# Fixing the order of ScalarE, VectorE and GpSimd in the expert part of an attention and mixture-of-experts kernel, with preparation in small lots

## The chip, the core and the metric

The kernel runs on one NeuronCore of a Trainium2 chip. The metric is the device time of one execution in microseconds (us). The engines are called as the profile calls them: PE (TensorE matrix multiply), PEld (its weight loads), DVE (VectorE), ACT (ScalarE), POOL (GpSimd) and SP (SyncE, whose queue issues every DMA here). "Lnnn" is a line of the kernel before, unless it is said to be of the changed one.

## What is computed

The reference chains three blocks on 1152 tokens (2 batches of 576) with width 512:

```python
out = attention(q, k, v, M_prev, z_prev, beta)       # causal, 8 heads of 64, gated with a memory read
x = out.transpose(0, 2, 1, 3).reshape(1152, 512)
a, b = x @ w1, x @ w2                                # 512 -> 1024
x = (a * b @ w3) @ w_out                             # 1024 -> 1024 -> 512
...
p = domain_probs / (domain_probs.sum(-1, keepdims=True) + 1e-09)
for e in range(4):                                   # the expert part
    h = np.maximum(x @ moe2_w1[e], 0.0)              # 512 -> 1024
    out += p[:, e:e + 1] * (h @ moe2_w2[e])          # 1024 -> 512
```

## The kernel before

Every matrix is split into a high half (rounded to the matmul format) and a low half (what is left), and a product is three matmul passes: high by low, low by high, high by high. ACT makes high halves (`hi`, a CAST), POOL or DVE the low halves (`lo_pool`, line 80; `lo_dve`, line 83, a subtraction).

The expert part is a loop over 32 steps: expert e (4), column block c (the 1152 tokens in two blocks, 2x320 and 2x256 columns), and a quarter j of the 1024 hidden features. `step(s, segs)` makes the first layer of a quarter by a seven-product scheme on 2x2 blocks. Its products write three PSUM tiles, Z, Q and R. In order: Z (A11 by B11), R (A12 by B21), Z again (S2 by T2), half of Q (S1 by T1), Z (S3 by T3), the other half of Q, Z (A22 by T4), Q (S4 by B22). Between them ACT copies Z out (s1, u2, u3), since the next product adds onto the same bank, and DVE adds the parts (t11, t22, t12). `relu_split` then makes the two halves of the hidden tile he: the high half on ACT, the low half on DVE. For A22 by T4 both halves are read from the Z bank itself, so the next step's first product waits for DVE's low half there. Between the products stand five segments of other PE work: in step 0 the last matmuls of the block before (`c1_rest`, L507), in all others the second layer of the step before (`layer2`, the matmuls into o, L741, 30 of them after a 320 block and 24 after a 256 block, and after each fourth quarter the additions into acc on DVE).

Work that has to be ready ahead of a step:

- `combine_x(c)`: the sums T1 to T4 of the tokens' blocks and the halves of T1 to T4 and B22, on ACT and DVE. For c = 0 it is needed from step 0's third product on, for c = 1 from step 4 on.
- `prep_1(s)`: the first layer's weights of step s. The raw tile r1 (two buffers) is loaded by `load_1` from SP, POOL forms sums in place (`s31`, `s24`, four operations of 256 columns), ACT and POOL make the halves `hi`/`lo` of four tiles w10 to w13: A11 and A12 in w10, S2 and S4 in w11, S1 and A22 in w12, S3 in w13.
- `prep_2(s)`: the second layer's weights w2, two `hi` on ACT and two `lo` on DVE, from r2, loaded by `load_2`.

What sets the order: only PE keeps the order of the program text (`manual_schedule` with PE alone). For ACT, DVE, POOL and SP the framework's scheduler lists each engine's instructions by its own estimate when the kernel is built; on the chip each engine then works through its list in order. The text feeds preparation through a queue (`pop`, line 779): up to four items after each segment, items for up to two steps ahead. The normalisation of the probabilities (10 small loads into `pr`, four DVE operations, L837 to L841) stands at the start of the expert part.

Of the kernel before, what the change touches and what calls it, by code (L numbers as in the profile page):

```python
# [33 lines left out]
def kernel(  # L34
# [34 lines left out]
    GAPB = 648  # L69
# [543 lines left out]
    def prep_1(s):  # L613


        if s >= len(steps):
            return []
# [29 lines left out]
        return [begin, hi(0), lo(0), s31, s24, hi(1), hi(2), lo(1), hi(3), lo(2), lo(3)]  # L647

    def prep_2(s):
        if s >= len(steps):  # L650
            return []
        st = {}

        def begin():
# [5 lines left out]
        return [  # L660
            begin,
            *(lambda x=x: nc.scalar.copy(w2s[s][x][:, 0], st["r"][:, x]) for x in range(2)),  # L662
            *(lambda x=x: lo_dve(w2s[s][x][:, 1], st["r"][:, x], w2s[s][x][:, 0]) for x in range(2)),
        ]
# [48 lines left out]

    def rows_of(t):

        c, i = divmod(t, TILES)
        t0, w = COLS[c]
        spans = []
        for b in range(B):
            lo, hi = max(i * P, b * w), min((i + 1) * P, (b + 1) * w)  # L720
            if lo < hi:
                spans.append((lo - i * P, hi - i * P, b * S + t0 + lo - b * w))
        return spans
# [51 lines left out]
    queue = []  # L775

    later = []

    def pop(s, n):
        while n and queue and queue[0][0] <= s + 2:  # L780
            queue.pop(0)[1]()
            n -= 1
        if later:
            later.pop(0)()

# [110 lines left out]
```

## Time and profile before

| | |
|---|---|
| time, median of 3 runs (lowest, highest) | 752.51 us (752.22, 752.82) |
| the profiled execution: its time, its span | 753.2 us, 751.4 us |
| granted TensorE clock, mean over the span | 0.991 |
| share of the span busy: PE, PEld, DVE, ACT, POOL | 96%, 86%, 56%, 51%, 48% |
| the chain that ended last, by engine | PE 83%, ACT 4%, DVE 4%, POOL 3%, DMA 3%, issue 2% |
| DMA | 73.55 MB, mean 98 GB/s |

The profiled execution's time is 1.8 us more than its span, and 0.7 us above the median. A granted clock of 1 stands for 2.4 GHz and 0.5 for 1.2 GHz. Matmuls are pipelined and their ends are modelled, so a share of 96% does not say that PE is at its peak; the length of a step, from the first product of one to that of the next, is the surer measure.

### The profile page before, as it was taken

To read this page: it belongs to the slowest core of one execution; us is meant where nothing else is said; L and a number is where in the kernel's file an instruction comes from. 1 tells how busy PE (TensorE), PEld (TensorE's weight loads), DVE (VectorE), ACT (ScalarE), POOL (GpSimd) and SP (SyncE) were. 2 spreads that over 40 slices of the span, in tenths; PEclk is the share of its full clock that TensorE was granted. 3 is DMA by queue.
4 is the path that set the end of the run, shared out by engine and by line. 5 is a ranking of instruction groups with operands and counts; after the bars stand their busy time and mean duration, and the time that the engine had idled before them with its cause. 6 is when DMAs were issued, how large, how long until landed. Compare 5 with 4: busy or idle time off the path is not lost.

```text
span 751.4 us, 12578 instructions
## 1 busy us (share of the span) xinstructions
PE 721.1 (96%) x4760; PEld 649.4 (86%) x4760; DVE 420.7 (56%) x824; ACT 382.6 (51%) x801; POOL 357.8 (48%) x356
## 2 busy tenths in 40 slices
PE   3899999999999999998988999999999999999998
PEld 2678888899999999998877989998999989999896
DVE  6987557566744125346774655536455464554633
ACT  7976557565734324334644554545545455454421
POOL 2174543534550016004388776556766557655500
PEclk9989999999999999999999999999999999999999
DMA  9873313443420012101252223222232323323201
GB/s 266 285 228 115 105 49 103 156 143 126 150 79 29 1 56 86 57 29 57 60 166 85 84 86 113 81 87 81 89 113 80 90 74 94 113 78 92 68 4 56
DMA packets 82716, 73.55 MB, mean 98 GB/s; under 512 B 16992, under 2 KB 66144, under 8 KB 82656
## 3 DMA queue, kind: packets, MB, share of 16 engines
q1 hardware_dynamic: 82656, 72.76, 31.7%
q8 instruction: 37, 0.61, 0.3%
q14 instruction: 23, 0.19, 0.1%
HBM read 66.19 MB, written 6.55 MB: 97 GB/s over the span
## 4 chain that ended last, share of the span: by engine, by line
PE 83%; ACT 4%; DVE 4%; POOL 3%; DMA 3%; issue 2%; SPq 0%; POOLq 0%; ACTq 0%; DVEq 0%
PE o L741 24%; PE ab L443 13%; PE Z L799 12%; PE Q L799 6%; PE a L268 6%; PE c L507 6%; PE wacc L378 5%; PE pt L255 3%; PE sc L215 3%; PE R L799 3%; DMA r<-in_moe_w_dram 2%; POOL w L80 2%; PE b L292 1%; DMA qd<-in_qT_dram 1%; ACT P L228 1%
## 5 line engine op out<-in xcount | busy, mean ns | idle before, releaser
L741 PE MATMUL o<-w,he 128*128 128x512 f32 x864 | 224.1, 393 | 0.0
L80 POOL TENSOR_TENSOR w<-r,w 128x512 fp32r<-128x512 f32 x96 | 131.6, 1375 | 136.1 <-ACT w L632 135.9
L741 PEld LDWEIGHTS o<-w,he 128*128 128x128 f32 x864 | 154.1, 189 | 23.6
L443 PE MATMUL ab<-xT,ws 128*128 128x288 f32 x768 | 111.1, 298 | 0.2 <-DVE asb L494 0.2
L443 PEld LDWEIGHTS ab<-xT,ws 128*128 128x128 f32 x768 | 103.4, 188 | 2.2 <-ACT w L632 0.4
L727 DVE SCALAR_TENSOR_TENSOR he<-t,he 128x320 fp32r<-128x320 f32 (+1 forms) x96 | 74.3, 774 | 40.2 <-ACT he L726 40.2
L632 ACT CAST w<-r 128x512 fp32r<-128x512 f32 x96 | 59.0, 619 | 53.8 <-PE Q L799 29.7
L726 ACT ACTIVATE he<-t 128x320 fp32r<-128x320 f32 (+1 forms) x96 | 42.6, 444 | 41.7 <-DVE t L812 22.9
L799 PE MATMUL Z<-X0T,w 128*128 128x320 f32 x288 | 51.7, 316 | 9.0 <-ACT u L820 3.8
L799 PEld LDWEIGHTS Z<-X0T,w 128*128 128x128 f32 x288 | 46.3, 191 | 14.6 <-ACT u L820 4.6
L83 DVE TENSOR_TENSOR w<-r,w 128x512 fp32r<-128x512 f32 x64 | 53.7, 861 | 8.3 <-ACT w L662 8.2
L507 PE MATMUL c<-hT,W 128*128 128x288 f32 (+2 forms) x384 | 56.1, 299 | 0.4 <-DVE hT L83 0.4
L268 PEld LDWEIGHTS a<-v,pT 114*120 114x120 f32 (+1 forms) x480 | 52.2, 185 | 2.8 <-issue 1.5
L268 PE MATMUL a<-v,pT 114*120 114x65 f32 (+1 forms) x480 | 53.6, 268 | 0.0
L507 PEld LDWEIGHTS c<-hT,W 128*128 128x128 f32 x384 | 52.3, 190 | 1.1 <-PE ab L443 0.6
L822 DVE TENSOR_TENSOR t<-u,Q 128x320 f32<-128x320 f32 (+1 forms) x32 | 14.5, 454 | 68.9 <-ACT u L820 68.9
L378 PE MATMUL wacc<-wo,w3s 128*128 128x512 f32 x192 | 50.9, 414 | 0.8 <-POOL w3s L77 0.7
L215 PE MATMUL sc<-ks,qs 64*120 64x120 f32 (+5 forms) x288 | 38.1, 377 | 12.1 <-POOL ks L80 9.5
L228 ACT ACTIVATE P<-P,mn 120x120 f32<-120x120 f32 (+3 forms) x80 | 42.6, 581 | 6.6 <-DVE mn L221 6.4
L799 PEld LDWEIGHTS Z<-X1T,w 128*128 128x128 f32 x288 | 40.7, 188 | 4.8 <-ACT u L816 1.0
L378 PEld LDWEIGHTS wacc<-wo,w3s 128*128 128x128 f32 x192 | 36.5, 197 | 9.2 <-issue 0.9
L215 PEld LDWEIGHTS sc<-ks,qs 64*120 64x120 f32 x288 | 25.0, 210 | 21.1 <-POOL ks L80 9.8
(120 smaller groups left out, 1197.4 us busy)
## 6 DMA issues: line engine op xcount, KB each, us to landing
r<-in_moe_w_dram SPq DMA_DIRECT2D x128, 256.0 KB, 3.7
wr<-in_moe_w_dram SPq DMA_DIRECT2D x16, 512.0 KB, 3.6
w3r<-in_moe_w3T_dram SPq DMA_DIRECT2D x16, 512.0 KB, 3.5
wor<-in_moe_w_out_dram SPq DMA_DIRECT2D x8, 512.0 KB, 6.8
wf<-tf SPq DMA_DIRECT2D x16, 256.0 KB, 2.2
wr<-wf SPq DMA_DIRECT2D x16, 256.0 KB, 2.8
v<-in_v_dram SPq DMA_DIRECT2D x16, 150.0 KB, 3.9
qd<-in_qT_dram SPq DMA_DIRECT2D x8, 288.0 KB, 3.6
```

Of the source, the lines that this page charges most:

```text
L80: nc.gpsimd.tensor_sub(dst, src, r32(hi))
L83: nc.vector.tensor_sub(dst, src, r32(hi))
L215: nc.tensor.matmul(ps[x][:, c : c + k1 - k0], lhsT=qs[o, a, q0[i] : q0[i] + RP], rhs=ks[o, b, k0:k1], start=(m == 0), stop=(m == 2),)
L228: nc.scalar.activation(Pt[i], Pt[i], AF.Exp, bias=mn[:, i : i + 1], scale=-1.0)
L268: nc.tensor.matmul(st["a"][:, x, i, :], lhsT=pt[x, i, j][0 : rows[j]], rhs=vn[0 : rows[j], j, :], start=(j == 0), stop=(j == i),)
L378: nc.tensor.matmul(wacc[t], lhsT=w3s[u][:, a, c, :], rhs=wo[4 * g + c][:, bb, :], start=(g == 0 and c == 0 and x == 0), stop=(g == 1 and c ...
L443: nc.tensor.matmul(ps[:, 0:HS], lhsT=self.ws[u][:, wi, kk, :], rhs=xT[b, kk][:, xi, a * HS : (a + 1) * HS], start=(n == 0), stop=(n == 3 * ...
L507: nc.tensor.matmul(st["ps"], lhsT=Wt[kk][:, wi, d * P : (d + 1) * P], rhs=hT[kk][:, xi, t0 : t0 + tw], start=(kk == 0 and x == 0), stop=(k ...
L632: return lambda: nc.scalar.copy(st["w"][i][:, 0], src(i))
L727: nc.vector.scalar_tensor_tensor(out=h[:, 1], in0=src, scalar=0.0, in1=r32(h[:, 0]), op0=ALU.max, op1=ALU.subtract)
L741: nc.tensor.matmul(o_ps[i], lhsT=h_of[s][x][:, a, i * P : (i + 1) * P], rhs=w2s[s][x][:, b, :], start=first, stop=last,)
L799: nc.tensor.matmul(ps, lhsT=w1s[s][a][:, wi, kk, :], rhs=X[c, b][:, xi, kk, :], start=first and kk == 0 and x == 0, stop=(kk == 1 and x == ...
```

## The change

`manual_schedule` now names PE, ACT, DVE and POOL: on all four the program's own order holds through the 32 steps. The queues are gone. Each step is handed two lists of five: `segs` (PE work, as before) and `after` (preparation, emitted after each segment). In step s the lots are `prep_1(s + 1)` and `prep_2(s)`, so preparation is one step ahead of its use, not up to two. `combine_x(0)` is emitted in a new order in step 0's first segment, `combine_x(1)` in seven pairs in the segments 0, 2 and 4 of steps 1 to 3. The probabilities' part moves into a function `norm_p`, called much earlier in the text, with `pr` and `prs` in the pool `main`; two paddings keep the tiles behind at the same offsets modulo 256 bytes.

```diff
@@ prep_1, prep_2: dictionaries of named pieces in place of lists @@
-        return [begin, hi(0), lo(0), s31, s24, hi(1), hi(2), lo(1), hi(3), lo(2), lo(3)]
+        return {
+            "s31": s31, "s24": s24, "begin": begin,
+            **{f"{n}{i}": f(i) for i in range(4) for n, f in (("hi", hi), ("lo", lo))},
+        }
...
+        return {"begin": begin, "hi0": hi(0), "hi1": hi(1), "lo0": lo(0), "lo1": lo(1)}
@@ combine_x @@
-            lambda: sub(t, b12, b11), lambda: sub(b11, b22, t), s2[0], lambda: sub(b12, b22, b12), *s2[1:],
-            s1[0], s3[0], lambda: sub(b21, b21, b11), *s1[1:], *s3[1:], *s4, *split_x("B22", c, b22),
+            [lambda: sub(t, b12, b11), s5[0]], [lambda: sub(b11, b22, t), s5[1]], [s2[0], lambda: sub(b12, b22, b12)],
+            [s1[0], s2[1], lambda: sub(b21, b21, b11)], [s3[0], s1[1]], [s4[0], s3[1]], [s4[1]],
@@ the loop of b1's units @@
         if u == 1:
             load_1(0), load_1(1)
+            norm_p()
@@ step @@
         def seg():
-            for f in segs.pop(0):
+            for f in (*segs.pop(0), *after.pop(0)):
                 f()
-            pop(s, 4)
@@ the loop over the steps @@
-    with tc.manual_schedule(engines={mybir.EngineType.PE}):
-        for f in prep_1(1):
-            f()
...
+    first = [g[0][0], g[1][0], *g[2], *g[3], g[4][1], g[4][0], *g[5], *g[6], g[0][1], g[1][1]]
+    rest = combine_x(1)
...
+    with tc.manual_schedule(engines={ET.PE, ET.Activation, ET.DVE, ET.Pool}):
         for s in range(len(steps)):
             load_1(s + 2)
+            after = [[] for _ in range(5)]
+            q = prep_2(s)
+            if s + 1 < len(steps):
+                p = prep_1(s + 1)
+                after[0] += [p["begin"], p["s31"], p["hi0"], p["lo0"]]
+                after[1] += [p["s24"], p["hi2"], p["lo2"]]
+                after[2] += [p["hi3"], p["lo3"]]
+                after[3] += [p["hi1"], p["lo1"]]
             if s == 0:
-                step(s, segs)
-                queue += [(0, f) for f in (*prep_2(0), *prep_2(1))]
-                later += combine_x(1)
-                pop(0, 5)
+                for n in ("begin", "s31", "hi0", "lo0", "s24"):
+                    p[n]()
+                segs[0] = first + segs[0]
+                after = [
+                    [], [p["hi1"], p["lo1"]], [q["begin"], q["hi0"], q["hi1"]], [q["lo0"], q["lo1"]],
+                    [p["hi2"], p["lo2"], p["hi3"], p["lo3"]],
+                ]
             else:
+                after[1] += [q["begin"], q["hi0"]]
+                after[2] += [q["hi1"], q["lo0"]]
+                after[3] += [q["lo1"]]
                 load_2(s + 1)
-                step(s, cut(layer2(s - 1), 5))
-                queue += [(s + 1, f) for f in prep_2(s + 1)]
-            queue += [(s + 2, f) for f in prep_1(s + 2)]
+                segs = cut(layer2(s - 1), 5)
+                for i in (0, 2, 4):
+                    if rest:
+                        after[i] += rest.pop(0)
+            step(s, segs, after)
```

PE's list is the same before and after, but for one attention matmul near its start. The other lists differ in the expert part. In names, w13_5 is tile 3 of step 5's first-layer weights, w2_1_0 is half 0 of step 1's second-layer weights, r1_5 and r2_1 the raw tiles they come from; the last number is a buffer's.

ACT in step 2, from the copy s1 to the copy u3, before:

```order
L810 COPY s1_2_4329<-Z2_4324 128x320
L632 CAST w11_3_4382<-r1_3_4182 128x512
L632 CAST w10_4_4512<-r1_4_4318 128x512
L726 ACTIVATE he2_0_4327<-t11_2_4332 128x320
L816 COPY u2_2_4330<-Z2_4324 128x320
L632 CAST w10_5_4642<-r1_5_4449 128x512
L820 COPY u3_2_4331<-Z2_4324 128x320
```

and in the changed kernel:

```order
L812 COPY s1_2_4330<-Z2_4325 128x320
L740 ACTIVATE he2_0_4328<-t11_2_4333 128x320
L633 CAST w10_3_4359<-r1_3_4182 128x512
L564 CAST X1T1_3236<-t3_3241 128x512
L818 COPY u2_2_4331<-Z2_4325 128x320
L633 CAST w12_3_4361<-r1_3_4182 128x512
L663 CAST w2_2_0_4390<-r2_2_4185 128x512
L822 COPY u3_2_4332<-Z2_4325 128x320
```

In step 2 the copy u3 stood behind a cast of step 5's raw tile; now it stands behind casts of step 3's and step 2's.

DVE in step 0, the sums and low halves of `combine_x(0)` ahead of the products that use T1 to T4, before:

```order
L574 TENSOR_TENSOR t3_3238<-x2_10_148,x2_00_146 128x640
L574 TENSOR_TENSOR x2_00_146<-x2_11_149,t3_3238 128x2x320
L574 TENSOR_TENSOR x2_10_148<-x2_11_149,x2_10_148 128x2x320
L83 TENSOR_TENSOR X0B22_3230<-x2_11_149,X0B22_3230 128x640
L575 TENSOR_TENSOR x2_01_147<-x2_01_147,x2_00_146 128x2x320
L83 TENSOR_TENSOR X0T1_3226<-t3_3238,X0T1_3226 128x640
L83 TENSOR_TENSOR X0T2_3227<-x2_00_146,X0T2_3227 128x640
```

and in the changed kernel:

```order
L578 TENSOR_TENSOR t3_3241<-x2_10_151,x2_00_149 128x640
L578 TENSOR_TENSOR x2_00_149<-x2_11_152,t3_3241 128x2x320
L578 TENSOR_TENSOR x2_10_151<-x2_11_152,x2_10_151 128x2x320
L83 TENSOR_TENSOR X0T2_3230<-x2_00_149,X0T2_3230 128x640
L579 TENSOR_TENSOR x2_01_150<-x2_01_150,x2_00_149 128x2x320
L83 TENSOR_TENSOR X0T1_3229<-t3_3241,X0T1_3229 128x640
```

The low half of T2, which step 0's third product reads, moves from seventh place to fourth, and that of B22, read by the last product, from fourth to the end.

DVE in step 1, from t22 to t12, before:

```order
L822 TENSOR_TENSOR t22_1_4197<-u3_1_4195,Q1_4189 128x320
L83 TENSOR_TENSOR w2_2_0_4357<-r2_2_4185,w2_2_0_4357 128x512
L727 SCALAR_TENSOR_TENSOR he1_1_4192<-t22_1_4197,he1_1_4192 128x320
L83 TENSOR_TENSOR w2_2_1_4358<-r2_2_4185,w2_2_1_4358 128x512
L727 SCALAR_TENSOR_TENSOR he1_1_4192<-Z1_4188,he1_1_4192 128x320
L83 TENSOR_TENSOR w2_3_0_4488<-r2_3_4321,w2_3_0_4488 128x512
L829 TENSOR_TENSOR t12_1_4198<-u2_1_4194,Q1_4189 128x320
```

and in the changed kernel:

```order
L824 TENSOR_TENSOR t22_1_4197<-u3_1_4195,Q1_4189 128x320
L741 SCALAR_TENSOR_TENSOR he1_1_4192<-t22_1_4197,he1_1_4192 128x320
L83 TENSOR_TENSOR w2_1_0_4254<-r2_1_3962,w2_1_0_4254 128x512
L578 TENSOR_TENSOR x2_00_149<-x2_11_152,t3_3241 128x2x256
L83 TENSOR_TENSOR X1B22_3240<-x2_11_152,X1B22_3240 128x512
L741 SCALAR_TENSOR_TENSOR he1_1_4192<-Z1_4188,he1_1_4192 128x320
L83 TENSOR_TENSOR w2_1_1_4255<-r2_1_3962,w2_1_1_4255 128x512
L831 TENSOR_TENSOR t12_1_4198<-u2_1_4194,Q1_4189 128x320
```

Between t22 and the low half that reads the Z bank there stand four operations now, where there were three; two of the four are of `combine_x(1)`. On SP the ten small loads into `pr` move from the head of the expert part to the attention part: five stand ahead of the load of `wor6` and five ahead of that of `wor7`, the raw tiles of w_out. DVE's four operations on them stand among the conversions of w_out.

## Rows read from the trace of the kernel before

**Rows 1.** The page's first part: busy us, share of the span, instructions

```profile
PE 721.1 (96%) x4760; PEld 649.4 (86%) x4760; DVE 420.7 (56%) x824; ACT 382.6 (51%) x801; POOL 357.8 (48%) x356
```

**Rows 2.** Windows of the expert part: stretch, length, engines' busy us, PEclk, DMA share, GB/s

```profile
343.00:470.50 127.50, 117.91 (x704) 106.47 (x703) 82.07 (x116) 66.77 (x147) 88.41 (x85) 0.97 0.32 96
470.50:564.60 94.10, 94.10 (x554) 85.13 (x553) 50.38 (x81) 46.95 (x104) 60.98 (x65) 1.00 0.30 90
```

**Rows 3.** Timeline, PE: first products of steps 1 to 6, then 9, 10

```profile
367.71 1.09 PE L799 MATMUL Z<-X0B,w 128*128 128x320 f32 x6
...
382.51 1.05 PE L799 MATMUL Z<-X0B,w 128*128 128x320 f32 x6
...
398.63 1.05 PE L799 MATMUL Z<-X0B,w 128*128 128x320 f32 x6
...
415.71 0.87 PE L799 MATMUL Z<-X1B,w 128*128 128x256 f32 x6
...
427.56 0.87 PE L799 MATMUL Z<-X1B,w 128*128 128x256 f32 x6
...
438.05 0.87 PE L799 MATMUL Z<-X1B,w 128*128 128x256 f32 x6
...
471.55 1.04 PE L799 MATMUL Z<-X0B,w 128*128 128x320 f32 x6
...
484.58 1.05 PE L799 MATMUL Z<-X0B,w 128*128 128x320 f32 x6
```

**Rows 4.** Timeline, PE: products that start late, with the idle time before them

```profile
356.83 1.97 PE L799 MATMUL Z<-X0T,w 128*128 128x320 f32 x6 [3.09 <-DVE X0T L83]
...
375.23 1.15 PE L799 MATMUL Z<-X0T,w 128*128 128x320 f32 x6 [1.45 <-ACT u L816]
...
394.03 1.15 PE L799 MATMUL Z<-X0T,w 128*128 128x320 f32 x6 [1.73 <-ACT u L820]
...
409.51 1.15 PE L799 MATMUL Z<-X0T,w 128*128 128x320 f32 x6 [2.07 <-ACT u L820]
...
443.35 0.97 PE L799 MATMUL Z<-X1T,w 128*128 128x256 f32 x6 [0.56 <-ACT u L816]
```

**Rows 5.** Timeline, step 3: SP's issue of raw tiles, ACT's cast ahead of u3

```profile
404.38 2.42 SPq L588 DMA_DIRECT2D r<-in_moe_w_dram  x4
...
408.52 0.62 ACT L632 CAST w<-r 128x512 fp32r<-128x512 f32 x1 [4.10 <-DMA r<-in_moe_w_dram]
```

**Rows 6.** Timeline, DVE in step 0: the last sum of combine_x(0)

```profile
353.42 1.89 DVE L575 TENSOR_TENSOR x<-x,x 128x640 f32<-128x640 f32 x1
```

**Rows 7.** Timeline, POOL and DVE side by side, in step 1 and in step 14

```profile
371.27 1.74 POOL L80 TENSOR_TENSOR w<-r,w 128x512 fp32r<-128x512 f32 x1
...
371.77 1.59 DVE L727 SCALAR_TENSOR_TENSOR he<-t,he 128x320 fp32r<-128x320 f32 x1
...
374.28 1.88 DVE L83 TENSOR_TENSOR X1T<-x,X1T 128x512 fp32r<-128x512 f32 x3
...
540.95 0.74 POOL L640 TENSOR_TENSOR r<-r 128x256 f32<-128x256 f32 x1
...
541.06 0.42 DVE L727 SCALAR_TENSOR_TENSOR he<-Z,he 128x256 fp32r<-128x256 f32 x1 [0.67 <-ACT he L726]
```

**Rows 8.** Timeline, a steady step from 565.63 on: POOL's two kinds, ACT's high half

```profile
571.02 0.74 POOL L639 TENSOR_TENSOR t<-r 128x256 f32<-128x256 f32 x1 [1.33 <-DMA r<-in_moe_w_dram]
...
573.60 0.47 ACT L726 ACTIVATE he<-t 128x320 fp32r<-128x320 f32 x1 [0.30 <-DVE t L822]
...
578.26 1.30 POOL L80 TENSOR_TENSOR w<-r,w 128x512 fp32r<-128x512 f32 x1 [0.69 <-ACT w L632]
```

**Rows 9.** Timeline: SP's loads of w_out, ACT's use of them, SP's small loads

```profile
17.72 3.65 SPq L346 DMA_DIRECT2D wor<-in_moe_w_out_dram  x3
...
26.75 1.20 ACT L103 ACTIVATE tf_wo<-wor 128x512 f32<-128x512 f32 x2
...
363.63 5.19 SPq L837 DMA_DIRECT2D pr<-in_moe_domain_probs_dram  x10
```

More of the change, by code (lines that the diff above doesn't have):

```diff
@@ L68 @@
     SHIFT = 8
-    GAPB = 648
+    GAPB = 640
     MASK = 8.0e9
@@ L87 @@
     gl = main.tile([P, H], F32, name="gl")
+    pr = main.tile([P, NTT, E], F32, name="pr")
+    prs = main.tile([P, NTT], F32, name="prs")
+    main.tile([P, SHIFT], F32, name="gapm")
     Wt = [main.tile([P, 2, DM], F32R, tag=f"u{t}", name=f"W{t}") for t in range(KF)]
@@ L613, in prep_1 @@
     def prep_1(s):
-        if s >= len(steps):
-            return []
         st = {}
@@ L658, in begin, with hi, lo, rows_of @@
             ]
[L660 to L664, printed above, removed]
+        def hi(x):
+            return lambda: nc.scalar.copy(w2s[s][x][:, 0], st["r"][:, x])
+        def lo(x):
+            return lambda: lo_dve(w2s[s][x][:, 1], st["r"][:, x], w2s[s][x][:, 0])
+        return {"begin": begin, "hi0": hi(0), "hi1": hi(1), "lo0": lo(0), "lo1": lo(1)}
+    TILES = 5
+    def rows_of(t):
+        c, i = divmod(t, TILES)
+        t0, w = COLS[c]
+        spans = []
+        for b in range(B):
+            lo, hi = max(i * P, b * w), min((i + 1) * P, (b + 1) * w)
+            if lo < hi:
+                spans.append((lo - i * P, hi - i * P, b * S + t0 + lo - b * w))
+        return spans
+    def norm_p():
+        for t in range(NTT):
+            for p0, p1, r0 in rows_of(t):
+                nc.sync.dma_start(out=pr[p0:p1, t, :], in_=probs[r0 : r0 + p1 - p0, :])
+        nc.vector.reduce_sum(out=prs, in_=pr, axis=AX.X)
+        nc.vector.tensor_scalar_add(prs, prs, 1e-9)
+        nc.vector.reciprocal(prs, prs)
+        nc.vector.tensor_mul(pr, pr, prs.unsqueeze(2).to_broadcast([P, NTT, E]))
     new_h(1)
     early = [f for k, n in enumerate(("B11", "B21")) for c in range(2) for f in split_x(n, c, block(0, k, c))]
-    early += prep_1(0)
+    p0 = prep_1(0)
+    early += [p0[n] for n in ("begin", "hi0", "lo0", "s31", "s24", "hi1", "hi2", "lo1", "hi3", "lo2", "lo3")]
     for u in range(NU):
@@ L694 @@
     WM = COLS[0][1]
-    TILES = 5
-    pr = pB.tile([P, NTT, E], F32, name="pr")
-    prs = pB.tile([P, NTT], F32, name="prs")
     acc4 = pB.tile([P, 1, DM], F32, name="acc4")
@@ L712 @@
     acc = [acc[t // 2][:, t % 2, :] for t in range(NTT)]
[L714 to L723, printed above, removed]
     def relu_split(h, src):
@@ L773, in cut, with step @@
         return [fs[k[i] : k[i + 1]] for i in range(n)]
[L775 to L784, printed above, removed]
-    def step(s, segs):
+    def step(s, segs, after):
         e, c, j = steps[s]
@@ L831, in step @@
         seg()
-    for f in combine_x(0):
-        f()
-    for t in range(NTT):
-        for p0, p1, r0 in rows_of(t):
-            nc.sync.dma_start(out=pr[p0:p1, t, :], in_=probs[r0 : r0 + p1 - p0, :])
-    nc.vector.reduce_sum(out=prs, in_=pr, axis=AX.X)
-    nc.vector.tensor_scalar_add(prs, prs, 1e-9)
-    nc.vector.reciprocal(prs, prs)
-    nc.vector.tensor_mul(pr, pr, prs.unsqueeze(2).to_broadcast([P, NTT, E]))
-    with tc.manual_schedule(engines={mybir.EngineType.PE}):
-        for f in prep_1(1):
-            f()
-        k = (0, 9, 12, 14, 16, 16)
-        segs = [c1_rest[k[i] : k[i + 1]] for i in range(5)]
+    g = combine_x(0)
```

6 lines of the change are left out of this document (4 added, 2 removed).

## The prediction

> **What bounds the kernel now.** I read the page's busy shares first, then the expert part in windows, then the timeline of PE step by step, and last what ACT, DVE and POOL were doing at the places where PE stood. PE is busy for 96% of the span [rows 1], so the question is where the rest is and who could give it back. The windows answer it for the expert part: from 470.50 to 564.60, eight steps, PE is busy for all 94.10 us, while in the first 127.5 us it lacks 9.6 us and its clock averages 0.97 [rows 2]. From step 8 on no order of the other engines can make PE faster; an order can only spoil it. What can be won lies in steps 0 to 7.
>
> Step lengths show it better, since they hold slow matmuls too. A 320-column step with nothing in its way takes 484.58 - 471.55 = 13.03 us. Steps 1, 2 and 3 take 14.80, 16.12 and 17.08 us [rows 3]: 1.77, 3.09 and 4.05 too long, 8.91 in sum. A 256-column step takes 438.05 - 427.56 = 10.49 us.
>
> The late products [rows 4] name the reasons. In step 0 PE waits 3.09 us for DVE's half of T2, and the six matmuls after it take 1.97 us where six after a shorter wait take 1.15. In step 1 it waits 1.45 us for u2, in steps 2 and 3 1.73 and 2.07 us for u3, in step 6 0.56 us for u2. Step 3 shows why u3 was late: the raw tiles were issued at 404.38, ACT took up a cast of one of them and stood 4.10 us until it had landed, at 408.52, and the copy u3 was queued behind that cast [rows 5].
>
> **What the change takes away.** *Step 0.* The half of T2 moves from seventh to fourth place on DVE. In the way before were the half of B22, the half of T1 and a sum that took 1.89 us [rows 6]. An undisturbed operation of DVE on 512 columns takes 0.63 us (three in 1.88 us [rows 7]), so about 0.8 on 640. The sums start at 349.2, as before, because they wait for PE. Three sums and one half then end near 352.7, before PE has finished the segment, at 356.83 - 3.09 = 353.74. T1's half ends near 354.3, and the product that reads it starts a 320-column product (0.9 us) after 353.7. So the 3.09 goes, and with it the slow matmuls: 1.97 - 1.15 = 0.8 on the first six, and for the 21 after them, which are still in part slow, I put 0.5. Together 4.4.
>
> *Steps 1 to 3.* ACT's casts are now of tiles one step ahead. The raw tile of step s + 2 is free when the last lot of step s has been made, late in step s - 1. From the issue at 404.38 to the cast at 408.52 is 4.1 us [rows 5], so it lands about 5 us into step s, and POOL and ACT want it from the end of that step on: some 5 us to spare in a short step, 8 in a long one. In front of u3 only casts of landed tiles remain: the waits of 1.73 and 2.07 go, and what followed the latter. The wait for u2 in step 1 came from DVE's three low halves and sums of block 1 ahead of the sum that ACT waited for; they are dealt out over steps 1 to 3. All 8.91 goes, as far as no new wait comes.
>
> *Step 6.* 0.56 of the same kind; DVE's w2 halves no longer stand ahead of t11. Sum of what goes: 4.4 + 8.9 + 0.6 = 13.9.
>
> **What it adds.** *Turns between POOL and DVE.* In step 1 of before, DVE's low half started at 371.77 while POOL's operation ran from 371.27 to 373.01, and it ended at 373.36: it waited and then ran its 0.4. But a low half that reads the Z bank took 0.42 in the middle of a POOL operation (541.06 in 540.95 to 541.69) [rows 7]. So where both operands lie in SBUF, the two engines take turns; with one in PSUM they don't. POOL's kinds take 0.74 and 1.30 us [rows 8]. By the Trainium skill ("SBUF — State Buffer", "SBUF: two separate sides") the port pair that VectorE and GpSimd share is an exclusive lock for a whole instruction and the loser blocks fully; it states no turns.
>
> *Step 1 is where this costs.* Its own tiles w12 and w13 are made only after step 0's last product, and POOL's lots for step 2 queue behind them. DVE has four operations between t22 and the half that reads the Z bank: the half of he, one of w2, a sum and the half of B22. In a steady step ACT's half after t22 ends at 573.60 + 0.47, which is 8.4 us into the step that starts at 565.63 [rows 8]; here about 8.7, as u3 waits a little behind a cast that needs POOL's sum. With turns: 8.7 + 0.4 + 1.3 + 0.6 + 0.7 + 0.6 + 1.3 + 0.6 + 0.45 = 14.65, and the next step's first product wants the bank at 13.03. PE waits 1.6 us. Nothing excludes less (POOL may be done earlier: 0) or more: if POOL kept its whole run first and its next sum too, 1.5 later, 3.1. I take 1.6. By the lock of that page with no turns it would be the 3.1, and the sum below would be 1.5 higher. In step 2 the same count has two operations fewer and ends about 13.2: 0.2.
>
> *Steady steps.* In 320-column steps DVE's late halves have over 2 us to spare. In 256-column steps POOL's operations that take turns are five of 0.74 and three of 1.30, 7.6 us, and DVE's three of 0.42 and two of 0.63, 2.5: together 10.1 of 10.49. It fits, with little left. The low bound is nothing; the high one is the loop that runs when every turn goes against DVE (POOL's lots and DVE's halves in alternation, then t12, the half of he, t11, ACT's half and the cast that starts POOL's next lot), which I count at 11.0, or 0.5 us a step. Coming out of a long step the chain has slack that shrinks by some 0.2 us a step, four steps in a row; I take 0.5 in all. DVE's additions into acc read PSUM and take no turns.
>
> *Front.* The ten loads cost SP 5.19 us [rows 9], 0.52 each: 2.6 us ahead of the load of wor6, 5.2 ahead of wor7. These went out from 17.72 on, and ACT read them from 26.75 on without a stop [rows 9], so up to 9 us lie between, of which the landing takes its share. DVE's four small operations come into a stretch in which it has hardly a gap, about 0.8 us. Bounds 0 and 3; I take 0.5, since ACT's list there runs about 1 us behind DVE's. In the expert part the loads' and the operations' removal wins nothing by itself.
>
> **The sum.** 13.9 - 1.6 - 0.2 - 0.5 - 0.5 = 11.1. From the profiled execution's 753.2 that gives 742.1; it was 0.7 above the median, so the forecast is 741.4.
>
> **Rivals.**
> *Turns in every short step.* If the loop of 11.0 holds in the 12 short steps that follow a short one, 6 us are given back: 747; in all 16, 8 us: 749. For it speaks the 10.1 of 10.49; against it that before does the same operations in the same time and waited but once for it, 0.56. Chance 0.17, at 744 to 750.
> *The front.* The small loads hold the w_out tiles back until ACT stands, up to 3 us: 744. For it: ACT and DVE are full there. Against it: the 9 us. Chance 0.1, at 743 to 745.
> *Slower: a step's casts meet the loads.* With one step of lead in place of two, ACT's first cast of step s + 1 stands ahead of u2, and if its tile lands late, PE stands for u2 each time. The price is that of step 3: 2.07 us per time. From six such steps on (6 x 2.07 = 12.4 against 11.1) the kernel is slower; in half of the 29 it would be 770. Against it speak the 5 to 8 us to spare. Chance 0.05.
> *Forecast.* 738.5 (nothing new is lost) to 744, chance 0.65; 0.03 is left for the change coming out even by a mix.
>
> **How the numbers follow.** 0.2% of 752.5 is 1.5 us, about what a measurement of this kernel can tell from no change. All of the first two rivals and the forecast are faster by more: 0.92. Same 0.03, slower 0.05. The range takes in the forecast, the front and most of the turns: 738 to 748.5, which leaves about 0.1 out at the top. The likeliest case's own range is 738.5 to 744.
>
> **What would show it.** Right: the first product of step 1 some 4.4 us earlier after step 0's start; steps 2 and 3 of 13.0 to 13.3 us; a wait of PE before step 2's first product, put down to DVE's half that reads Z; no ACT cast that waits for a DMA ahead of a u copy; steps 8 to 31 as long as before. Wrong: PE idle time behind u2 or behind the Z bank in the 256-column steps, a first expert product later than 343.6 by more than a microsecond, or a T2 half that still ends after 353.7.

## The result, and the profile after

The changed kernel takes 741.33 us in the median (740.95 to 741.67, 4 runs) against 752.66 us before; the ratio is 0.984, with a 95% interval of 0.982 to 0.986. The forecast was 741.4. That the sum came out to 0.1 us is in part luck: some of its terms were wrong, and their errors cancel.

The profiled execution of the changed kernel takes 741.36 us, its span is 739.5 us, 11.9 less than before. The page's first part, as in [rows 1]:

```profile
PE 717.3 (97%) x4760; PEld 648.3 (88%) x4760; DVE 410.1 (55%) x824; ACT 380.6 (51%) x801; POOL 364.5 (49%) x356
```

The windows of the expert part, the same two stretches as in [rows 2] (length, engines' busy us, granted clock, DMA share, GB/s):

```profile
343.00:470.50 127.50, 126.58 (x778) 116.11 (x778) 77.60 (x119) 67.11 (x149) 80.50 (x78) 1.00 0.28 83
470.50:564.60 94.10, 94.10 (x554) 85.13 (x553) 49.65 (x82) 46.48 (x104) 64.35 (x65) 1.00 0.31 90
```

In the first stretch PE lacks 0.9 us where it lacked 9.6, and its granted clock is 1.00 where it was 0.97; the second, eight steps, is full as before. The 0.9 is one wait, the only one that PE's timeline shows in the whole expert part. The timeline of PE, first products of steps 0 to 4:

```profile
344.82 1.05 PE L802 MATMUL Z<-X0B,w 128*128 128x320 f32 x6
...
364.26 1.05 PE L802 MATMUL Z<-X0B,w 128*128 128x320 f32 x6
...
378.37 1.15 PE L802 MATMUL Z<-X0B,w 128*128 128x320 f32 x6 [0.92 <-DVE he L741]
...
391.55 1.04 PE L802 MATMUL Z<-X0B,w 128*128 128x320 f32 x6
...
404.63 0.87 PE L802 MATMUL Z<-X1B,w 128*128 128x256 f32 x6
```

Step 0 of the kernel before starts here; its later steps are in [rows 3]:

```profile
343.59 1.05 PE L799 MATMUL Z<-X0B,w 128*128 128x320 f32 x6
```

Differences of such starts give the steps of both kernels, in us:

| | before | changed | gain |
|---|---|---|---|
| start of step 0 | 343.59 | 344.82 | -1.23 |
| step 0 | 24.12 | 19.44 | 4.68 |
| steps 1, 2, 3 | 14.80, 16.12, 17.08 | 14.11, 13.18, 13.08 | 0.69, 2.94, 4.00 |
| step 6 | 11.31 | 10.48 | 0.83 |
| all others and the tail | | | none over 0.02 |

The gains add up to 13.14, and 13.14 - 1.23 = 11.91 is the difference of the spans.

A part of these gains is PE's granted clock. In the kernel before it fell from 1.00 to 0.50 (from 2.4 to 1.2 GHz) twice in the expert part, each time for 3.4 us: in step 0 toward the end of PE's wait of 3.09 us, and in step 3, 1.5 us after a wait of 2.07 us had ended. The windows of these two stretches, before:

```profile
356.46:359.86 3.40, 3.03 (x12) 3.03 (x13) 2.44 (x5) 0.94 (x2) 0.00 (x0) 0.50 0.00 0
411.07:414.47 3.40, 3.40 (x12) 3.01 (x11) 1.00 (x3) 1.36 (x3) 3.18 (x6) 0.50 0.00 0
```

PE's 3.0 and 3.4 us in them would have taken half as long at 1.00. So, as an estimate from these rows, 1.5 us of step 0's gain and 1.7 us of step 3's are the clock. In the changed kernel it stays at 1.00 from step 0 to the last 1.1 us of the span.

The wait of 0.92 us is the one that was forecast, and DVE and POOL in step 1 show how it comes about (timeline, both engines):

```profile
372.73 0.64 DVE L741 SCALAR_TENSOR_TENSOR he<-t,he 128x320 fp32r<-128x320 f32 x1 [0.54 <-ACT he L740]
...
372.98 1.54 POOL L80 TENSOR_TENSOR w<-r,w 128x512 fp32r<-128x512 f32 x1
373.29 1.78 DVE L83 TENSOR_TENSOR w<-r,w 128x512 fp32r<-128x512 f32 x1
...
374.49 1.18 POOL L80 TENSOR_TENSOR w<-t,w 128x256 fp32r<-128x256 f32 x1
375.00 1.22 DVE L578 TENSOR_TENSOR x<-x,t 128x512 f32<-128x512 f32 x1
...
375.63 1.74 POOL L80 TENSOR_TENSOR w<-r,w 128x512 fp32r<-128x512 f32 x1
...
376.14 1.78 DVE L83 TENSOR_TENSOR X1B<-x,X1B 128x512 fp32r<-128x512 f32 x1
377.33 1.17 POOL L640 TENSOR_TENSOR t<-r 128x256 f32<-128x256 f32 x1
377.84 0.48 DVE L741 SCALAR_TENSOR_TENSOR he<-Z,he 128x320 fp32r<-128x320 f32 x1
```

Where both engines have work, their operations end in turn: w2's half on DVE ends 0.55 us after POOL's half, POOL's next 0.60 after that, and so on. The half that reads Z ends at 378.32, and PE's product starts at 378.37.

### The profile page after: what moved, and what is told of

It reads as the page before. It is cut to its first block, busy times and chain, and to the rows that moved or that the text cites. A ratio compares the mean times of both kernels' runs of the same rounds, so it can differ in the third digit from the quotient of the medians.

```text
span 739.5 us, 12497 instructions
## 1 busy us (share of the span) xinstructions
PE 717.3 (97%) x4760; PEld 648.3 (88%) x4760; DVE 410.1 (55%) x824; ACT 380.6 (51%) x801; POOL 364.5 (49%) x356
## 4 chain that ended last, share of the span: by engine, by line
PE 90%; DVE 3%; ACT 2%; DMA 2%; SPq 1%; issue 1%; POOL 0%; DVEq 0%; ACTq 0%
PE o L755 26%; PE Z L802 14%; PE ab L446 13%; PE Q L802 7%; PE c L510 7%; PE a L271 6%; PE wacc L381 5%; PE R L802 3%; PE sc L218 3%; PE pt L258 3%; DMA qd<-in_qT_dram 2%; PE b L295 1%; SPq L147 1%; ACT P L231 1%; PE x L314 1%
## 5 line engine op out<-in xcount | busy, mean ns | idle before, releaser
L741 DVE SCALAR_TENSOR_TENSOR he<-t,he 128x320 fp32r<-128x320 f32 (+1 forms) x96 | 57.0, 593 | 49.1 <-ACT he L740 49.1
L83 DVE TENSOR_TENSOR w<-r,w 128x512 fp32r<-128x512 f32 x64 | 67.0, 1048 | 0.0
L271 PEld LDWEIGHTS a<-v,pT 114*120 114x120 f32 (+1 forms) x480 | 53.7, 189 | 3.4 <-issue 1.7
L271 PE MATMUL a<-v,pT 114*120 114x65 f32 (+1 forms) x480 | 55.1, 271 | 0.3 <-DVE mn L224 0.3
L802 PE MATMUL Z<-X0T,w 128*128 128x320 f32 x288 | 50.2, 310 | 0.0
L258 PE MATMUL pt<-identF,P 120*120 120x120 f32 x240 | 38.8, 288 | 4.4 <-ACT pT L260 2.4
```

Of the source, the lines that this page charges most:

```text
L83: nc.vector.tensor_sub(dst, src, r32(hi))
L258: nc.tensor.transpose(ps[:, sl], Pt[i][:, q0[j] : q0[j] + RP], identF[0:RP, 0:RP])
L271: nc.tensor.matmul(st["a"][:, x, i, :], lhsT=pt[x, i, j][0 : rows[j]], rhs=vn[0 : rows[j], j, :], start=(j == 0), stop=(j == i),)
L741: nc.vector.scalar_tensor_tensor(out=h[:, 1], in0=src, scalar=0.0, in1=r32(h[:, 0]), op0=ALU.max, op1=ALU.subtract)
L802: nc.tensor.matmul(ps, lhsT=w1s[s][a][:, wi, kk, :], rhs=X[c, b][:, xi, kk, :], start=first and kk == 0 and x == 0, stop=(kk == 1 and x == ...
```

## The experiments

Three questions: which lists made the gain, where each stall had come from, and what the turns cost. Step lengths are compared within the expert part, each from one profile. The start of step 0 can't be compared so: ten profiles in which the lists ahead of the expert part are those of the changed kernel start it anywhere from 343.81 to 346.81, with a median of 345.9; three with the former lists there start it at 343.59, 343.77 and 344.05. This spread is in the first 63 us: PE's 241st matmul starts at 59.6 to 62.6 us in the ten, and from there to step 0 it is 284.0 to 284.3 us in every profile. The time of a kernel that ran once holds this spread, so it says little below some 3 us.

**The lots without the kept order.** One line differs:

```diff
-    with tc.manual_schedule(engines={ET.PE, ET.Activation, ET.DVE, ET.Pool}):
+    with tc.manual_schedule(engines={ET.PE}):
```

> The changed kernel with only PE's order kept, as before: the lots stand in the text, ACT, DVE and POOL are listed by the scheduler again. Theory (the kept order takes the waits of steps 0 to 3 away): the list of DVE shows B22's half again ahead of T2's and eight w2 halves drawn ahead, so steps 0 to 3 take about 72 us again (72.1 before, 59.8 changed), and the time is 750 to 753. Rival (preparation one step ahead in lots is enough, whatever lists it): steps 0 to 3 within 1.5 us of 59.8, time 741 to 743.

753.57 us in the median (751.55 to 756.78, 10 runs), ratio 1.000 (0.998 to 1.002) to the kernel before. Steps 0 to 3 take 24.29, 19.12, 13.44 and 13.61 us, 70.5 in sum. In the time, the lots by themselves are worth nothing. In steps 0 to 6 they are worth 1.5 us (104.2 against 105.8), about as much as the probabilities' part, which this kernel has too, costs ahead of them. The opposite, the kept order without the lots, was not run. Timeline of this kernel, DVE in step 1 and the product of PE that waits:

```profile
377.80 1.77 DVE L83 TENSOR_TENSOR w<-r,w 128x512 fp32r<-128x512 f32 x1
...
379.50 1.22 DVE L83 TENSOR_TENSOR X1T<-x,X1T 128x512 fp32r<-128x512 f32 x1
380.64 2.34 DVE L83 TENSOR_TENSOR w<-r,w 128x512 fp32r<-128x512 f32 x2
382.90 1.00 DVE L741 SCALAR_TENSOR_TENSOR he<-t,he 128x320 fp32r<-128x320 f32 x1
383.83 0.47 DVE L824 TENSOR_TENSOR t<-u,Q 128x320 f32<-128x320 f32 x1
...
384.36 1.17 PE L802 MATMUL Q<-X0B,w 128*128 128x320 f32 x6 [3.43 <-DVE t L824]
```

u3 was copied at 376.89; the sum t22 that needs it came 7 us later, behind four low halves that were not wanted yet, and PE stood 3.43 us.

**One engine's order at a time.** The same line with `{ET.PE, ET.DVE}` and with `{ET.PE, ET.Activation}`.

> The changed kernel with the order of PE and DVE kept, ACT and POOL listed by the scheduler. Theory (the waits of steps 1 to 3 came from casts that ACT's list holds ahead of the copies u2 and u3 and of the high halves): they come back, steps 1 to 3 take 45 to 50 us (48.0 before, 40.4 changed), step 0 stays under 21, time 746 to 752. Rival (DVE's kept order is enough): steps 1 to 3 within 1 us of 40.4, 741 to 743.

> The changed kernel with the order of PE and ACT kept, DVE and POOL listed by the scheduler. Theory (DVE and POOL can't run ahead of the casts that they follow, so ACT's order holds them too): steps 1 to 3 within 1.5 us of 40.4; in step 0 T2's half stands fifth on DVE, one place later, so step 0 takes 19.4 to 20.3; time 741 to 743.5. Rival (each of the three lists matters by itself): steps 0 to 3 take 63 us or more (59.8 changed), 745 or more.

DVE's order alone: 758.94 us, steps 1 to 3 take 47.2 us, step 0 21.17, a little over the 21 expected. ACT in step 3 of this kernel, and PE:

```profile
403.98 0.62 ACT L663 CAST w<-r 128x512 fp32r<-128x512 f32 x1 [3.76 <-DMA r<-in_moe_w_dram]
404.50 0.42 ACT L812 COPY s<-Z 128x320 f32<-128x320 f32 x1
...
404.98 1.15 PE L802 MATMUL Z<-X0T,w 128*128 128x320 f32 x6 [2.95 <-ACT s L812]
```

It is the picture of [rows 5]: a cast that waits for its load, a copy of Z behind it, PE behind the copy. The cast is of step 4's w2, whose load went out at 399.35, in step 3. The theory held for the waits, but the time is past its 752, because the short steps wait now too (steps 13 to 16 take 47.2 us where the changed kernel takes 43.2). ACT's order alone: the theory held for the place that it spoke of (steps 0 to 3 take 58.6 us, 1.2 less than in the changed kernel, since DVE's list happens to put other operations ahead of the Z half) and failed for the time: 756.39 us. The short steps broke, step 7 takes 14.11 us and step 15 15.11. POOL and ACT there, and PE:

```profile
433.60 0.74 POOL L640 TENSOR_TENSOR t<-r 128x256 f32<-128x256 f32 x1 [3.80 <-DMA r<-in_moe_w_dram]
...
440.37 0.62 ACT L633 CAST w<-r 128x512 fp32r<-128x512 f32 x1 [4.82 <-POOL r L646]
...
441.62 0.38 PE L802 MATMUL Z<-X1T,w 128*128 128x256 f32 x1 [1.14 <-ACT s L812]
```

POOL's list puts a sum of the tile after next ahead of the halves that are due, waits 3.80 us for that tile, and is then behind for the rest of the step. The last cast of the lots, of S2 and S4, should run in step 6; it waits 4.82 us for POOL's sum until 2.4 us into step 7, and with ACT's order kept the high half of t12 and the copy s1 can't pass it. So it takes more than one list: DVE's or ACT's alone gave 759 and 756 us, in one run each, and the kernel before 752.45 to 755.52 in nine runs beside them. POOL's order alone, and two of the three together, were not run.

**The order of the sums in step 0.** `first` in the order that ACT and DVE had before, B22's half fourth and T2's seventh; POOL's lots as changed:

```diff
-    first = [g[0][0], g[1][0], *g[2], *g[3], g[4][1], g[4][0], *g[5], *g[6], g[0][1], g[1][1]]
+    first = [g[0][0], g[0][1], g[1][0], g[3][0], g[2][1], g[2][0], g[1][1], g[4][0], g[3][2], g[4][1],
+             g[3][1], g[5][0], g[5][1], g[6][0]]
```

> The changed kernel with the sums and halves of the first token block in the order in which DVE and ACT had them before (T2's half seventh on DVE); POOL's lots stay where the change puts them. Theory of the prediction (T2's place on DVE made the 3.09 us wait): step 0 takes about 24 us again, time 746. Rival (half of it or more was POOL taking turns with the sums: they took 1.03 to 1.89 us before and take 0.82 now): seven operations of 0.75 us end 1 to 1.2 us later than the product wants, step 0 takes 20.5 to 21, time 742.5 to 743.

Step 0 takes 20.59 us: 1.15 more than in the changed kernel, where the kernel before takes 4.68 more. The step came out as the rival had it; the time of its single run, 744.32 us, holds a late start of step 0 (346.81). DVE in this kernel, from the first sum to T2's half, and PE:

```profile
352.39 0.82 DVE L578 TENSOR_TENSOR t<-x,x 128x640 f32<-128x640 f32 x1 [2.03 <-ACT x L515]
...
357.01 2.29 DVE L83 TENSOR_TENSOR X0T<-x,X0T 128x640 fp32r<-128x640 f32 x3
357.88 1.15 PE L802 MATMUL Z<-X0T,w 128*128 128x320 f32 x6 [0.91 <-DVE X0T L83]
```

T2's half is still seventh, but none of the operations is stretched: it starts 4.62 us after the first sum, where before it started 6.80 after (355.97 - 349.17). POOL is idle from 351.8 on here; before, it worked until 354.6 beside the sums, the last of which took 1.89 us [rows 6]. The timeline before, the first and the third sum, a half on POOL, and T2's half as the first of two:

```profile
349.17 1.03 DVE L574 TENSOR_TENSOR t<-x,x 128x640 f32<-128x640 f32 x1 [0.95 <-ACT x L512]
...
351.40 1.36 DVE L574 TENSOR_TENSOR x<-x,x 128x640 f32<-128x640 f32 x1
...
352.90 1.73 POOL L80 TENSOR_TENSOR w<-r,w 128x512 fp32r<-128x512 f32 x1 [0.82 <-ACT w L632]
...
355.97 1.54 DVE L83 TENSOR_TENSOR X0T<-x,X0T 128x640 fp32r<-128x640 f32 x2
```

With POOL quiet, the seventh place costs 0.91 us of waiting in place of 3.09; the other 2.2 took POOL's work as well. That does not split the wait in two: before, the third sum ended at 352.76, so a half in fourth place would have ended near 353.6 (an estimate, with the 0.82 us of a half), ahead of the 353.74 at which PE stood. The new place alone may have been enough. No run has it beside POOL's former work.

**The lot ahead of the Z half.** The second lot of `rest` goes to segment 3 of step 1, behind the half that reads Z:

```diff
-                        after[i] += rest.pop(0)
+                        after[3 if (s, i) == (1, 2) else i] += rest.pop(0)
```

> The changed kernel with one lot of step 1 (a sum and the low half of B22 of the second token block) moved one segment later, so that DVE makes the half that reads the Z bank ahead of both. Theory (the 0.92 us wait ahead of step 2's first product is those two operations, 1.15 and 1.70 us long by turns with POOL): the wait is gone, step 1 takes 13.0 to 13.1 us (14.11 now), time 740.2. Rival (POOL keeps the port for the half anyway): 0.4 us or more of the wait stays. Second rival: the lot now makes t12 late, and a wait of 0.5 us or more shows in step 2.

The wait of 0.92 is gone and step 1 takes 13.03 us, but step 2 takes 13.88 in place of 13.18. The second rival had that, though with 0.5 us or more of waiting. The two operations now stand ahead of t12, which comes at 377.98, 1.71 us after step 2's first product where a steady step has it at 0.20; ACT waits for it ahead of the copy s1, and PE 0.28 us for that. Steps 1 to 3 gain 0.34 us where 1.08 went. The lot was the cause; where it went it was one again. The single run took 740.01 us.

**Two steps ahead.** `prep_1` of step s + 2 in the lots from step 5 on, both in step 4:

```diff
-            if s + 1 < len(steps):
-                p = prep_1(s + 1)
+            for n in (s + 1,) if s < 4 else (s + 1, s + 2) if s == 4 else (s + 2,):
...
+                p = prep_1(n)
```

> The changed kernel with the same lots, but from step 5 on of the tiles two steps ahead (step 4 makes both), loads as they are. Theory (a cast of a tile two steps ahead meets its load, and whatever is queued behind it on ACT is late): the first cast of each step waits for the DMA until about 5 us into the step and stands ahead of u2, PE waits 0.7 to 2.5 us in nearly every step from 6 on: 760 to 800 us. Rival (the waits of before came from the order alone and not from the lead): no wait, 741 to 742.

747.83 us in its single run. What the expert part loses is in one place: step 5 takes 15.62 in place of 10.49, no other step is more than 0.06 longer. PE waits 2.15 us there for POOL, which makes two tiles in one step, and 1.52 and 0.67 for the copies u2 and u3. Timeline, ACT and PE in step 5, SP and ACT in step 6:

```profile
425.50 0.62 ACT L633 CAST w<-r 128x512 fp32r<-128x512 f32 x1 [4.04 <-DMA r<-in_moe_w_dram]
...
426.44 0.97 PE L802 MATMUL Z<-X1T,w 128*128 128x256 f32 x6 [1.52 <-ACT u L818]
...
435.30 0.93 SPq L592 DMA_DIRECT2D r<-in_moe_w_dram  x2
...
436.24 0.60 ACT L633 CAST w<-r 128x512 fp32r<-128x512 f32 x1
```

Both numbers fall, the theory's 760 to 800 and the rival's 741 to 742. ACT waits for a load twice, 0.35 us in step 4 and 4.04 in step 5, and not after. The wait comes while preparation gets ahead, when two tiles are made in one step and the second catches up with its load. Once it is two steps ahead, the raw tile's buffer comes free a step earlier too, the load goes out a step earlier (at 435.30 that of step 9's tile, whose lots stand in step 7), and no cast waits. In this run it is not the lead that costs but the moment in which a list draws ahead; steps 2 and 3 of before (3.74 and 4.10 us of waiting for a tile) look the same.

**More work for POOL.** `lo1` twice in every step from 4 on:

```diff
-                after[3] += [p["hi1"], p["lo1"]]
+                after[3] += [p["hi1"], p["lo1"], *([p["lo1"]] if s > 3 else [])]
```

> The changed kernel with one low half of 128x512 made twice on POOL in every step from 4 on (the same values written again), 1.3 us more of POOL per step. Theory of the prediction (turns with DVE fill 10.1 of a short step's 10.49 us): 11.4 us are wanted, each 256-column step gets 0.5 to 0.9 us longer, 12 to 16 of them, 748 to 755. Rival (the two engines have slack, since most of DVE's operations come while POOL is idle): no step longer by more than 0.1, 741 to 742.

No step is longer by more than 0.02 us (the median step of 256 columns takes 10.49 in both). Windows of step 13, first of the changed kernel:

```profile
510.56:521.05 10.49, 10.49 (x68) 9.47 (x66) 6.39 (x9) 5.56 (x13) 7.65 (x9) 1.00 0.36 100
```

and with the additional half:

```profile
511.95:522.43 10.48, 10.48 (x67) 9.47 (x66) 6.23 (x10) 5.56 (x13) 8.99 (x10) 1.00 0.34 101
```

POOL is busy for 8.99 of 10.48 us and PE has no gap. The rival held for the steps: the turns leave room. The single run took 743.19 us and starts step 0 at 346.21.

**The turns by themselves.** Behind the output, eight operations of 128x512 on DVE, alone and beside eight of POOL:

```diff
+        def both(i): nc.vector.tensor_sub(dd[:, i % 2], a, b)
+        def psum(i): nc.vector.scalar_tensor_tensor(out=dd[:, i % 2], in0=Zb, scalar=0.0, in1=b, op0=ALU.max, op1=ALU.subtract)
+        def one(i): nc.vector.tensor_scalar(out=dd[:, i % 2], in0=a, scalar1=1.0, scalar2=1.0, op0=ALU.mult, op1=ALU.mult)
+        for n, d, k in zip(BL, (both, both, psum, psum, one, one), (0, 8, 0, 8, 0, 8)):
...
+            for i in range(8): d(i)
+            for i in range(k): nc.gpsimd.tensor_sub(dp[:, i % 2], a, b)
```

> The changed kernel, and behind its output six stretches of eight DVE operations of 128x512, each alone and then beside eight subtractions of 128x512 on POOL: a subtraction with both operands in SBUF, one with an operand in PSUM, and a multiplication by 1 of one SBUF operand. Theory (turns for two SBUF operands, none with one in PSUM): alone 0.6 to 0.7 us each; beside POOL 1.8 to 2.0 for the first kind, POOL's at the same pace; 0.6 to 0.7 for the second, POOL at 1.3. Rival by an exclusive lock without turns: DVE's first kind waits until POOL's eight are over, or POOL's until DVE's are. For the operation with one SBUF operand the theory says nothing: 0.6 or less if it leaves the port alone, 1.8 to 2.0 if it takes turns. The time is longer by these stretches and is not compared.

The timeline of the stretches, eight operations in a row, DVE alone (L879, L882 and L885 for the first time), then beside POOL (L895), last POOL alone:

```profile
738.32 4.90 DVE L879 TENSOR_TENSOR X1T<-X1T,X1T 128x512 fp32r<-128x512 f32 x8
...
743.54 13.01 POOL L895 TENSOR_TENSOR X1T<-X1T,X1T 128x512 fp32r<-128x512 f32 x8
...
744.75 12.35 DVE L879 TENSOR_TENSOR X1T<-X1T,X1T 128x512 fp32r<-128x512 f32 x8
...
757.57 4.87 DVE L882 SCALAR_TENSOR_TENSOR X1T<-Zb,X1T 128x512 fp32r<-128x512 f32 x8
...
762.76 9.83 POOL L895 TENSOR_TENSOR X1T<-X1T,X1T 128x512 fp32r<-128x512 f32 x8
...
763.96 4.86 DVE L882 SCALAR_TENSOR_TENSOR X1T<-Zb,X1T 128x512 fp32r<-128x512 f32 x8
...
772.86 2.77 DVE L885 TENSOR_SCALAR X1T<-X1T 128x512 fp32r<-128x512 f32 x8
...
775.95 11.14 POOL L895 TENSOR_TENSOR X1T<-X1T,X1T 128x512 fp32r<-128x512 f32 x8
...
777.16 10.21 DVE L885 TENSOR_SCALAR X1T<-X1T 128x512 fp32r<-128x512 f32 x8
...
787.69 9.80 POOL L900 TENSOR_TENSOR X1T<-X1T,X1T 128x512 fp32r<-128x512 f32 x8
```

With both operands in SBUF, eight operations of DVE take 0.61 us each alone and 1.54 beside POOL, POOL's 1.23 alone and 1.63 beside DVE. These means hold a first operation on each engine that ran before the turns began; from then on each engine's operations start 1.67 us after one another (DVE's at 748.68 and 750.35, POOL's at 748.17 and 749.84). So they take turns, one for one, and a turn of both costs 1.67 us, less than the 0.61 + 1.23 = 1.84 of its parts and less than the 1.8 to 2.0 expected; some 0.2 overlap. The rival, one engine shut out until the other's eight are over, falls. With an operand in PSUM neither notices the other (4.86 against 4.87, 9.83 against 9.80). With one operand, in SBUF, DVE's goes from 0.35 to 1.28 in the mean and 1.40 in the turns (777.49, 778.89): it takes turns too.

**The probabilities.** In the first attempt only the call of `norm_p` was moved in the text, to the head of the expert part:

> The changed kernel with the ten small loads and four operations of the probabilities back at the head of the expert part. Theory (they cost the attention part 1.2 to 1.35 us, since the qd load stands behind them on SP and ACT waited 1.11 us for it): the first expert product starts at 343.6 in place of 344.8, the expert part is as long as now, time 740.1. Rival (the front's loss has another cause, the one attention matmul that moved or noise of the clock): first product at 344.5 to 345, time 741.0 to 741.6. Third: the loads get in the way of raw tiles at the head of the expert part, which gets longer by as much, 741.3 with a first product at 343.6.

The median is 742.22 us (740.25 to 743.52, 5 runs), and the edit did not do what it meant: the scheduler drew the loads back to where they were (SP issues the first five at 19.60), since nothing in the expert part kept them. The second attempt puts `pr` and `prs` into the expert part's pool again, with the former paddings, whose space is free only then; it was run beside the changed kernel.

```diff
-    pr = main.tile([P, NTT, E], F32, name="pr")
-    prs = main.tile([P, NTT], F32, name="prs")
-    main.tile([P, SHIFT], F32, name="gapm")
...
+    pr = pB.tile([P, NTT, E], F32, name="pr")
+    prs = pB.tile([P, NTT], F32, name="prs")
...
+    norm_p()
     g = combine_x(0)
```

> The changed kernel itself, timed again beside the next one. If the 1.23 us by which its first expert product started later (344.82 against 343.59) belong to the change, this profile shows 344.5 to 345 again and a median of 741 to 742; if the front varies by that much from one execution to the next (343.81, 344.48 and 346.81 were seen with the same lists up to there), the start may lie anywhere from 343.5 to 347.

> The changed kernel with the probabilities' part undone: pr and prs in the pool of the expert part again, loads and the four operations at its head, so the attention part has the lists of before. Theory (the ten small loads and four operations cost the front about 1.2 us): median 1.2 us, give or take 0.4, below that of the changed kernel on this chip. Rival (the front's difference was noise, or is given back at the head of the expert part): medians within 0.5 us of each other.

The changed kernel takes 741.70 us (740.26 to 742.81, 5 runs; its profile starts step 0 at 346.28), this one 740.10 (739.80 to 740.61, 4 runs; 343.77). Steps 0 to 3 take 59.7 us, and 59.8 in the changed one. The theory held, at the edge of its 0.8 to 1.6: the part costs about 1.6 us in the medians, all ahead of the expert part, though the two sets of runs overlap by 0.35 us. The timeline of the changed kernel shows one thing that comes later, SP, ACT and PE:

```profile
24.28 3.26 SPq L686 DMA_DIRECT2D pr<-in_moe_domain_probs_dram  x5
...
28.11 0.38 SPq L147 DMA_DIRECT2D qd<-in_qT_dram  x1
...
33.68 0.68 ACT L186 ACTIVATE ex<-qd 128x576 f32<-128x576 f32 x1 [1.11 <-DMA qd<-in_qT_dram]
...
36.42 1.05 PE L258 MATMUL pt<-identF,P 120*120 120x120 f32 x4 [1.53 <-ACT pT L260]
```

The load of qd goes out at 28.11, behind the small loads; before it went out at 22.41. ACT waits 1.11 us for it, and PE 1.53 for a copy further down ACT's list. That wait is not all loss, since PE stood for 1.21 and 0.66 us in the same stretch before. Between PE's 101st and 241st matmul, where the two profiles part, it idles 3.0 us in place of 2.3, and the rest of the 1.5 us by which this part is longer is slower matmuls: the granted clock is 0.50 for 10.2 us here, from 35.3 on, and before for 6.8, from 39.0 on. How much of the 1.6 is the loads, how much DVE's four operations and how much the clock was not separated.

**A version made from this.** The probabilities undone, and the nine DVE operations of the second token block one by one, each where DVE is idle:

```diff
+    g1 = combine_x(1)
+    rest = {
+        (1, 0): g1[0], (1, 1): g1[1][:1], (1, 4): [g1[2][0], g1[1][1]],
+        (2, 0): [g1[2][1], g1[3][0]], (2, 1): [g1[3][1]], (2, 4): [g1[4][0], g1[3][2]],
+        (3, 0): [g1[4][1], g1[5][0]], (3, 1): [g1[5][1]], (3, 4): g1[6],
+    }
...
-                for i in (0, 2, 4):
-                    if rest:
-                        after[i] += rest.pop(0)
+                for i in range(5):
+                    after[i] += rest.get((s, i), [])
```

> A version made from what was found: the probabilities undone as in the run before, and the nine DVE operations of the second token block one by one in the segments 0, 1 and 4 of steps 1 to 3, none between t22 and the half that reads Z. Theory: the 0.92 us wait goes, and no other comes, since DVE stood idle over 2 us in segment 1; steps 0 to 3 take 58.6 us (59.8 changed), 1.1 us less than with the probabilities undone alone: 739.0. Rival (the waits move, as in the run with B22 behind the Z half, where 1.08 us went and 0.7 came back): 739.5 to 740.2.

739.13 us (738.68 to 740.12, 5 runs), ratio 0.980 (0.979 to 0.982) to the kernel before. Steps 0 to 3 take 19.44, 13.03, 13.01 and 13.01 us, 58.5 in sum, and PE has no wait in the expert part. Its first window:

```profile
343.00:470.50 127.50, 127.50 (x784) 117.34 (x783) 82.10 (x125) 67.58 (x150) 82.42 (x79) 1.00 0.29 85
```

## Why the prediction came out, step by step

*Step 0* was put at 4.4 us and gave 4.68. T2's half came when it was forecast: it ended 8.95 us after the step's first product (352.95 + 0.82 - 344.82), and 9.1 had been worked out. With that the wait went, and the slow matmuls with it: put at 1.3 us, they were 1.59, most of it the stretch at a granted clock of 0.50, which the prediction did not name. What it left out is POOL. The row of 1.89 us stood in the text, and the turns were described for step 1, but were not applied to step 0: without POOL's work beside the sums the former order costs only 1.15 us. That the size came out so well owes something to luck, since POOL's quiet in step 0 was not counted on.

*Steps 1 to 3*: all 8.91 us went, less the new waits. That casts and copies queued behind work that was not due is shown by the run in which only DVE's order is kept; step 3's 4.05 us also held 1.7 of the lower clock. That a cast two steps ahead meets its load as a rule is not shown: in the run two steps ahead it did so only while preparation drew ahead. In step 1 one reading was wrong: the three low halves of 1.88 us [rows 7] start at 374.28, behind the sum t11 (373.88) that ACT waited for. Ahead of it stood two sums, the half of he and one low half, and the sums and the half of he took 1.79, 1.23 and 1.59 us in turns with POOL.

*Step 6* was put at 0.56 and gave 0.83: its late product started 0.73 us later than in the step before (the profile's idle time does not hold all of a delay, since it models the ends of matmuls), and the six matmuls took 0.10 longer.

*Turns in step 1* were put at 1.6 us and cost 1.08 (0.92 of it idle time in the profile). The mechanism was as said: w2's half, the sum and B22's half end 1.70, 1.15 and 1.70 us after one another. The term was mis-sized because the sum added POOL's and DVE's times in full, 1.9, 1.3 and 1.9; these 0.55 us are the difference, as the start came 0.2 earlier and the half of he took 0.2 longer than put down. Step 2 was put at 0.2 for a wait of the same kind and cost 0.15, but no such wait came: 0.10 of it are the six matmuls behind step 1's wait (1.15 us, where 1.05 is usual).

*Steady steps* were put at a loss of 0.5 us and lost nothing, and "it fits, with little left" was wrong: 1.3 us more of POOL per step fitted as well. The 10.1 of 10.49 added POOL's time to DVE's as if both stood in one chain. POOL prepares for a whole step later; its lateness costs nothing until a cast of ACT waits for it ahead of a copy, as with ACT's order alone kept. The rival of turns in every short step falls with it.

*The front* was put at 0.5 us with bounds 0 and 3. It cost 1.23 in the profile, about 1.6 in the medians. So one of the prediction's own signs of being wrong came, a first expert product more than a microsecond after 343.6. The load that came late was qd, which the prediction did not name; it looked at w_out's tiles alone, of which one was waited for, 0.47 us.

*The sum*: 11.1 forecast, 11.9 in the profiles. A loss too small by 0.7 (the front) stands against losses too large (0.5 in the steady steps, 0.5 in step 1) and gains too small (0.3 in step 0, 0.2 in step 6). Its closeness to the result is the luck of these signs. The rival that the kernel gets slower by casts that meet their loads did not come: PE waited for no copy in any step.

The rule quoted from the Trainium skill ("SBUF — State Buffer", "SBUF: two separate sides"), an exclusive lock for a whole instruction, agrees with the runs: in step 1 DVE's operations end 0.55 us after POOL's has ended, though they had been taken up before (at 373.29, 375.00 and 376.14). That the loser stays out for longer, which the prediction weighed at 3.1 us, does not follow from it and did not happen: in the measured stretch the engines alternate, one operation of each in 1.67 us. The same section names DVE operations with two SBUF inputs or in a two-port mode as those that need the pair; the stretches agree for two inputs, 1.54 with both in SBUF and no change with one in PSUM; that the one-input operation, 0.35 alone and 1.28 beside POOL, is in such a mode no run shows.

## What to carry to other kernels

Where engines work through their lists in order, an operation that is not due yet and has to wait holds up all behind it; look for the cast, sum or load that stands ahead of a copy that PE wants, and fix the order on all engines that feed each other: here three together gained 11 us, and DVE's or ACT's alone left the kernel slower than with none. Beside POOL, place DVE operations with operands in SBUF where DVE is idle, and count a pair of operations (1.67 us here) rather than each engine by itself. A part that a scheduler may move (here ten small loads) is part of the change, wherever it ends up.

## What had not been expected of the hardware

DVE's one-operand multiplication from SBUF to SBUF, the quickest of the three alone (0.35 us for 128x512), is the one that turns slow most: 1.40 us in turns with POOL, 4 times as long, where the subtraction of two SBUF operands goes from 0.61 to 1.67 and that with an operand in PSUM stays at 0.61. The span ahead of the expert part varied by 3.0 us over ten executions of the same lists, all of it in the first 63 us, while steps 8 to 30 repeated to 0.02 us wherever all three orders were kept. And a wait of PE cost more than its length where the granted clock fell as well: 3.09 us of waiting made step 0 4.68 us longer, and 0.91 us in the same place, with the clock at 1.00, 1.15.
